# Chunk attention and a bilinear layer on one core: DMA turns ahead of later loads, the sums of weights spread out, the start and block 0's outputs rearranged

## The chip, the cores and the metric

The kernel runs on one core of one Trainium2 chip. The metric is device time in microseconds (us); less is better. A run is one execution of the whole program, and the time given for a kernel is the median of its runs.

The names of the engines in the profile are PE (TensorE, matrix products; PEld are its weight loads), DVE (VectorE), ACT (ScalarE), POOL (GpSimd) and SP (SyncE, whose queue issues every DMA of this kernel).

## The reference

```python
scores = scale * np.matmul(q_c, k_c.transpose(0, 1, 2, 4, 3))   # q, k, v: (8, 8, 576, 64), chunks of 64
attn = np.exp(scores - np.max(scores, axis=-1, keepdims=True))
attn = attn / (np.sum(attn, axis=-1, keepdims=True) + 1e-09)
x = np.matmul(attn, v_c)   # back to (8 batches * 576, 8 heads * 64) = (4608, 512)
a = x @ w_a                # (512, 1536)
b = x @ w_b
out = (a * b) @ w_out      # (4608, 1536) @ (1536, 512), float32
```

Attention is within chunks of 64 positions. Its result, 4608 tokens of 512 values, goes through a layer in which two products are multiplied with each other.

## The kernel before

**Tiles.** The 4608 tokens are 9 blocks of 512 (`NBLK`), a block is two units of 256 tokens (`NU` = 18). Unit u belongs to block u // 2. Units 0 and 1 are done in a way of their own at the start ("half" and "quad" helpers).

**A unit's attention.** `load_natural` brings q, k and v as float32, half a MB each, to `f32[u % 3]`, in two DMAs for a tensor (four for units 8 and 9, whose chunks are of different batches). `cast_qk` and `cast_v` make bfloat16 on GpSimd (`qkb[u % 2]`, `vb[u % 3]`). Then q and k must be turned, so that the head dimension lies on the partitions: for most units by one DMA, `transpose_dma` (line 215), to `qkT[u % 3]`; for units 2 and 3 by TensorE products with the identity (`transpose_pairs`, line 193), with copies out of PSUM by VectorE (q) and ScalarE (k). On TensorE follow `scores` (line 233), `sums` (line 250) and `values` (line 266). ScalarE does the exponential (line 244), the logarithm of the sums (line 276) and the exponential of its negative (line 280); VectorE multiplies the two (`normalise`, line 285) into `xT`, three buffers by block.

**A slot.** `slot(uv, us)` (line 660) puts the sums and values of unit uv and the scores of unit us between the products of a block. What of it runs on ScalarE and VectorE waits in a list `late`, from which `step` takes one entry per step of the block and `drain` all.

**A block's layer.** `ffn(K, ft)` is one step: 4 products with `wb` and 4 with `wa` for one of 12 tiles of 128 columns (line 397), then a copy by ScalarE (line 408) and the product of both by VectorE (line 409). For block 1, steps 0 to 6 are done in halves, first for unit 2, then for unit 3. In blocks 0 and 1 each of four output tiles takes 12 products (line 419), a copy by VectorE (line 429) and a store (line 435). Blocks 2 to 8 use `outs_fast` (line 466) instead, seven products of half width in place of eight for a pair of tiles. It needs sums of the weights, made once on GpSimd by `sum_wo` (lines 453 to 456, six calls), and sums of the products, made by VectorE in each block (`sum_ab`, lines 462 to 464). Both are kept in the buffer `wsta`, through whose ten parts the weights were loaded: the sums of weights in parts 0 to 3, those of products in parts 4 to 7; output weights 0 to 5 lie in parts 4 to 9.

**Order.** The order of every engine's work is the order of the program, written out by hand from line 521 on; nothing reorders it. SP's queue takes loads, turns and stores in program order too; a DMA waits there for its buffer or its data, and all that follows waits with it. Around the change the program has, before: at the end of block 0 cast and turn of unit 4, k and v of unit 5, all of unit 6, cast of unit 5; the turn of unit 5 and the load of unit 7 in the first half steps of block 1; the turn of unit 6 and the load of unit 8 behind step 8, the turn of unit 7 and the load of unit 9 behind output tile 1. The slots are (3, none), (none, 4), (4, 5) behind step 10 of block 1, (5, 6) behind its output tile 1, and from block 2 on one behind step 1 and one behind step 8.

PSUM has four single banks F that `nextF` gives out in a ring, and the pairs PS (scores) and PA (values).

Of the kernel before, what the change touches and what calls it, by code (L numbers as in the profile page):

```python
# [11 lines left out]
def kernel(  # L12
# [10 lines left out]
    nc = tc.nc  # L23
# [11 lines left out]
    DM = H * D  # L35
# [71 lines left out]
    def nextF():  # L107
        return ring("f", F)
# [193 lines left out]
    def quad_cast(m, x, eng):  # L302
        c = (m % 2) * 512
        copy(
            eng,
            qkb[m // 2][:, x, c:c + 512].rearrange("p (r h d) -> p h r d", r=4, h=2),
            f32[m // 2][x][:, c:c + 512].rearrange("p (h r d) -> p h r d", h=2, r=4),
        )

    def quad_turn(m, x, eng):  # L310

        t = nextF().bitcast(BF16)
        c0 = (m % 2) * 512
        for r in range(4):
            c = r * 128
            nc.tensor.transpose(
                t[:, c:c + 128], qkb[m // 2][:, x, c0 + c:c0 + c + 128], identity
            )
        n = 8 * x + 4 * (m % 2)
        dst = qkT[m // 2][:, n:n + 4, :]  # L320
        if x == 0:
            copy(eng, dst, t[:, 0:512].rearrange("p (r t) -> p r t", r=4))
        else:
            copy(
                eng,
                dst.rearrange("p a b -> p (a b)").rearrange("p (t r) -> p t r", r=4),
                t[:, 0:512].rearrange("p (r t) -> p t r", r=4),
            )
# [95 lines left out]
            stop=(ft == NFT - 1),  # L424
        )

    def out_close(K, tg, o):
        t = ring("o", osb)
        nc.vector.tensor_copy(out=t, in_=o)  # L429
        store(K, tg, t)  # L430

    def store(K, tg, t):
        for p, n, b, s0 in runs(2 * K + tg // 2, tg % 2):
            r0 = b * S + s0
            nc.sync.dma_start(out=out[r0:r0 + n, :], in_=t[p:p + n, :])

    def outs(K, tgs):
        o = [nextF() for _ in tgs]
# [27 lines left out]
    def outs_fast(K, t):  # L466
        c = t * 128
        m3, m4, w, y1, y2 = [part[:, t, n, :] for n in range(5)]
        oa, ob = ring("o", osb), ring("o", osb)
        V, A, G = nc.vector, nc.scalar, nc.gpsimd  # L470

        def product(a, b, o=None, pairs=range(NP)):
            o = nextF()[:, 0:HF] if o is None else o
            for i in pairs:
                nc.tensor.matmul(  # L475
                    o, a(i)[:, c:c + 128], b(i), start=(i == 0), stop=(i == NP - 1)
                )
# [35 lines left out]
    def fill(n):  # L513

        for _ in range(n):
            nc.tensor.matmul(PA[:, 0, :], zero[:, 0:128], zero, start=True, stop=True)

    staged = {}

# [1 line left out]
    with tc.manual_schedule():  # L521
# [87 lines left out]
        half_sums(1, 1, PS)  # L609
        half_log(PS)  # L610
        half_inverse(1, 0)
        half_inverse(1, 1)
        cast_v(0, G, 2)
        half_values(0)
        for mm in range(2):
            half_normalise(0, mm)
        land_half("b", 0, 0, G)
# [12 lines left out]
        land_half("a", 0, 1, G)  # L630


        def load_unit(u, xs=(0, 1, 2)):
            if u < NU:
                for x in xs:
                    load_natural(u, x, (q, k, v)[x], nc.sync)

        def cast_unit(u, xs=(0, 1, 2)):
            if u < NU:
                for x in xs:  # L640
                    if x < 2:
                        cast_qk(u, x, G)
                    else:
                        cast_v(u, G)

        def turn_unit(u):
            if u < NU:
                transpose_dma(u, nc.sync)

        def turn_pairs(u, x, engs):  # L650
# [87 lines left out]
        out_close(0, 3, o)  # L738
        slot(None, 3, True)
        drain()  # L740
        cast_unit(4)
        turn_unit(4)
        load_unit(5, (1, 2))
        load_unit(6)
        cast_unit(5)

        for ft in range(7):
            step()
            ffn(1, ft, (0,))
            if ft == 1:  # L750
                slot(3, None, short=True)
            if ft == 3:
                turn_unit(5)
                load_unit(7)
        for ft in range(7):
            step()
            ffn(1, ft, (1,))
            if ft == 3:
                slot(None, 4)
                cast_unit(6)  # L760
        for ft in range(7, NFT):
            step()
            ffn(1, ft)
            if ft == 8:
                turn_unit(6)
                load_unit(8)
                sum_wo(1, G)
            if ft == 10:
                slot(4, 5)
                sum_wo(2, G)  # L770
                cast_unit(7)
        for tg in range(4):
            step()
            outs(1, (tg,))
            if tg == 1:
                slot(5, 6)
                turn_unit(7)
                load_unit(9)
                for i in range(3, NP):
                    sum_wo(i, G)  # L780
        for K in range(2, NBLK):
            for s in range(NFT + 2):
                step()
                if s < NFT:
                    ffn(K, s)
                    if s % 2:
                        sum_ab(s // 2)
                else:
                    outs_fast(K, s - NFT)
                for s0, u in ((1, 2 * K + 3), (8, 2 * K + 4)):  # L790
                    if s == s0 and u - 1 < NU:
                        slot(u - 1, u if u < NU else None)
                    if s == s0 + 1:
                        cast_unit(u + 1)
                    if s == s0 + 3:
                        turn_unit(u + 1)
                        load_unit(u + 3)


# [28 lines left out]
```

## Time and profile before

| | us |
|---|---|
| median of 8 runs | 326.84 |
| lowest, highest | 325.60, 329.06 |
| the profiled execution | 329.06 |
| its span in the trace | 327.3 |
| PE busy in it | 310.3 |
| DVE, ACT, POOL busy in it | 184.5, 132.9, 124.8 |

How to read the profile: a line of a timeline has the start in us, how long the group lasts, the engine, the line of the kernel, the operation, the operands and how many instructions the group has; in brackets stands the idle time of the engine just before, and what ended it. A line of the windows has for each stretch its length, each engine's busy time with the number of its instructions, the granted share of TensorE's clock, the busy share of the DMA engines and their GB/s. A line of a DMA queue (SPq) tells when the queue began with the DMA and how long it was busy issuing it; the data land later. The row of digits of the page has 40 slices of 8.2 us each.

### The profile page before, as it was taken

The numbers are of one execution on the slowest core, as the hardware profiler recorded it, in microseconds if no ns is written. First come the engines' busy times: TensorE is split into PE (matmuls) and PEld (weight loads), VectorE is DVE, ScalarE is ACT, GpSimd is POOL, SyncE is SP. The second block draws the span as 40 slices with busy tenths as digits, with TensorE's granted clock in tenths as the row PEclk, the third lists the DMA queues.
The fourth block names the chain that finished last, engine by engine and source line by source line (L and its number), as shares of the span: only waits on it lengthen the run. The fifth ranks groups of instructions, "written<-read, shape, count | busy, mean of one in ns | idle before, by whom it ended". The sixth has DMA issues, their size and how long they took to land.

```text
span 327.3 us, 7303 instructions
## 1 busy us (share of the span) xinstructions
PE 310.3 (95%) x2910; PEld 178.1 (54%) x2910; DVE 184.5 (56%) x369; ACT 132.9 (41%) x224; POOL 124.8 (38%) x161
## 2 busy tenths in 40 slices
PE   7599999996996999999999999999999999999994
PEld 3334446862442448644854485458545844684474
DVE  3433435532343566596569647875787467646662
ACT  3623216643144353356244614461546163513320
POOL 3657857327993302810281039003900400050022
PEclk9879999997897899999999999999999999999999
DMA  7999999999878999599159917991510110011003
GB/s 233 255 322 386 398 276 255 276 220 247 189 179 201 221 231 231 177 229 239 51 151 237 212 39 133 251 226 65 153 44 0 67 66 0 2 65 66 0 1 128
DMA packets 145698, 55.00 MB, mean 168 GB/s; under 512 B 126208, under 2 KB 139520, under 8 KB 145664
## 3 DMA queue, kind: packets, MB, share of 16 engines
q1 hardware_dynamic: 145664, 54.54, 65.6%
q8 instruction: 22, 0.36, 0.5%
q14 instruction: 12, 0.10, 0.1%
HBM read 37.75 MB, written 9.44 MB: 144 GB/s over the span
## 4 chain that ended last, share of the span: by engine, by line
PE 71%; DMA 13%; SPq 9%; POOL 3%; issue 1%; DVE 1%; POOLq 0%; DVEq 0%
PE F L397 46%; PE F L475 19%; SPq L123 5%; DMA wst<-in_moe_w_a_dram 5%; DMA f<-in_k_dram 3%; DMA f<-in_v_dram 2%; SPq L153 2%; PE F L419 2%; DMA qkT<-qkb 2%; PE PS L233 1%; PE F L250 1%; DMA f<-in_q_dram 1%; SPq L146 1%; PE PA L266 1%; POOL wst L453 1%
## 5 line engine op out<-in xcount | busy, mean ns | idle before, releaser
L397 PE MATMUL F<-xT,wb 128*128 128x512 bf16 (+1 forms) x460 | 116.3, 375 | 0.9 <-DVE xT L383 0.9
L397 PE MATMUL F<-xT,wa 128*128 128x512 bf16 (+1 forms) x460 | 115.3, 373 | 0.2 <-POOL wa L171 0.2
L409 DVE TENSOR_TENSOR ab<-F,bsb 128x512 bf16<-128x512 f32 (+1 forms) x115 | 75.3, 656 | 63.8 <-PE F L397 57.2
L408 ACT CAST bsb<-F 128x512 bf16<-128x512 f32 (+1 forms) x115 | 64.0, 558 | 113.8 <-PE F L397 112.8
L397 PEld LDWEIGHTS <-wa 128*128 128x128 bf16 x460 | 45.4, 99 | 50.8 <-issue 3.6
L397 PEld LDWEIGHTS <-wb 128*128 128x128 bf16 x460 | 44.4, 99 | 47.1 <-issue 4.1
L493 POOL TENSOR_TENSOR part<-part 128x256 f32<-128x256 f32 x14 | 10.1, 724 | 144.6 <-ACT part L501 144.6
L171 POOL CAST qkb<-f 128x1024 bf16<-128x1024 f32 (+1 forms) x37 | 35.5, 975 | 23.3 <-DMA f<-in_q_dram 12.3
L475 PEld LDWEIGHTS <-wst 128*128 128x128 bf16 x420 | 41.1, 98 | 4.8
L475 PE MATMUL F<-wst 128*128 128x256 bf16 x252 | 33.6, 273 | 0.0
L285 DVE TENSOR_TENSOR xT<-PA,inv 128x512 bf16<-128x512 f32 x32 | 21.8, 684 | 15.2 <-ACT inv L280 15.2
L493 DVE TENSOR_TENSOR osb<-F,part 128x256 f32<-128x256 f32 x56 | 22.3, 420 | 10.7 <-POOL part L493 10.4
L171 POOL CAST vb<-f 128x1024 bf16<-128x1024 f32 (+2 forms) x22 | 20.2, 919 | 11.4 <-DMA f<-in_v_dram 8.8
L493 POOL TENSOR_TENSOR part<-part,osb 128x256 f32<-128x256 f32 x28 | 19.7, 725 | 12.2 <-DVE osb L493 12.2
L276 ACT ACTIVATE lns<-F 128x512 f32<-128x512 f32 x32 | 17.4, 595 | 15.8 <-PE F L250 15.8
L419 PE MATMUL F<-wo,ab 128*128 128x512 bf16 x96 | 22.9, 390 | 0.6 <-DVE osb L429 0.6
L475 PE MATMUL F<-wst,ab 128*128 128x256 bf16 x168 | 22.9, 273 | 0.0
L244 ACT ACTIVATE E<-PS 128x1024 bf16<-128x1024 f32 (+1 forms) x20 | 18.8, 941 | 6.6 <-PE PS L339 4.0
L463 DVE TENSOR_TENSOR wst<-ab 128x512 bf16<-128x512 bf16 x42 | 20.9, 498 | 0.0
L464 DVE TENSOR_TENSOR wst<-ab 128x512 bf16<-128x512 bf16 x42 | 20.9, 497 | 0.0
L475 PE MATMUL F<-wo,wst 128*128 128x256 bf16 x168 | 20.6, 273 | 0.0
L493 DVE TENSOR_TENSOR part<-F,part 128x256 f32<-128x256 f32 x14 | 5.9, 425 | 22.7 <-POOL part L493 22.7
(49 smaller groups left out, 194.4 us busy)
## 6 DMA issues: line engine op xcount, KB each, us to landing
out_dram<-osb SPq DMA_DIRECT2D x32, 256.0 KB, 2.2
f<-in_q_dram SPq DMA_DIRECT2D x28, 256.0 KB, 4.1
f<-in_k_dram SPq DMA_DIRECT2D x28, 256.0 KB, 4.1
f<-in_v_dram SPq DMA_DIRECT2D x28, 256.0 KB, 4.7
wst<-in_moe_w_out_dram SPq DMA_DIRECT2D x6, 512.0 KB, 8.8
wst<-in_moe_w_b_dram SPq DMA_DIRECT2D x5, 512.0 KB, 8.4
wst<-in_moe_w_a_dram SPq DMA_DIRECT2D x5, 512.0 KB, 8.4
f<-in_v_dram SPq DMA_DIRECT2D x16, 128.0 KB, 3.3
```

What stands on the lines that cost most here:

```text
L171: eng.tensor_copy(out=out, in_=in_)
L244: nc.scalar.activation(out=e[:, :, s], in_=PS[:, :, s], func=AF.Exp, scale=scale)
L276: nc.scalar.activation(out=lns[:, cl, :], in_=SU[cl], func=AF.Ln)
L285: nc.vector.tensor_tensor(out=x.rearrange("p m (g c t) -> p c g m t", g=2, c=2)[:, cl], in0=PA[:, cl, :].rearrange(shape, g=2, m=4), in1=i ...
L397: nc.tensor.matmul(bank[:, 0:n], w[ft // 2][ft % 2][:, kt, :], x[:, kt, us[0] * 256:us[0] * 256 + n], start=(kt == 0), stop=(kt == NKT - 1),)
L408: nc.scalar.copy(out=bT[:, 0:n], in_=banks[0][:, 0:n])
L409: nc.vector.tensor_tensor(out=ab[ft][:, us[0] * 256:us[0] * 256 + n], in0=banks[1][:, 0:n], in1=bT[:, 0:n], op=MULT)
L419: nc.tensor.matmul(o, ab[ft][:, tg * 128:(tg + 1) * 128], wo[ft // 2][:, ft % 2, :], start=(ft == 0), stop=(ft == NFT - 1),)
L463: nc.vector.tensor_tensor(out=y[:, 0:2], in0=a[:, 0:2], in1=a[:, 2:4], op=ADD)
L464: nc.vector.tensor_tensor(out=y[:, 2:4], in0=a[:, 1:3], in1=a[:, 0:4:3], op=SUB)
L475: nc.tensor.matmul(o, a(i)[:, c:c + 128], b(i), start=(i == 0), stop=(i == NP - 1))
L493: eng.tensor_tensor(out=out, in0=in0, in1=in1, op=op)
```

## The change

- The loads of a unit are split on SP's queue: q of the next unit goes first, then the DMA turn of the unit before it, then k and v. This holds for the turns of units 5 to 8. The four stores of block 0 go behind the turn of unit 4 and k and v of unit 5.
- The slots move: (none, 4) by one half step forward; (5, 6) is split into (5, none) behind output tile 0 of block 1 and (none, 6) behind step 0 of block 2; in block 2, (6, 7) stands behind step 4 and (7, 8) behind step 9.
- The sums of weights: 0 and 1 behind slot (none, 4), ahead of the casts of unit 6; 2 and 3 ahead of the casts of unit 8; 4 and 5 behind cast and turn of unit 8.
- In block 0's outputs the turns of units 2 and 3 by TensorE stand within the products of tiles 2 and 3, and slot (none, 2) behind tile 2.
- At the start, inverse, values and normalising of the first half unit stand ahead of the sums of the second, and four matmuls on zeros (`fill`) to a spare bank are added.
- In the last block the last tile pair's second store is split in two halves of 256 columns; the first half is stored as soon as it is there.

The core of the diff:

```diff
@@ outs_fast
+        halves = K == NBLK - 1 and t == 1
+        if halves:
+            store(K, 2 + t, ob, 0, HF)
...
-        store(K, 2 + t, ob)
+        store(K, 2 + t, ob, HF if halves else 0)
@@ start
         expo(1, 0)
+        half_inverse(0, 0)
+        half_inverse(0, 1)
...
+        cast_v(0, G, 2)
+        land_half("b", 0, 0, G)
         quad_scores(3)
         expo(1, 1)
-        half_inverse(0, 0)
-        half_inverse(0, 1)
+        half_values(0)
+        for mm in range(2):
+            half_normalise(0, mm)
         half_sums(1, 0, PS)
...
+        spare = F[2]
+        fill(1, spare)
         ffn_products(0, 0, (0, 1), (0, 1), B0, "b")
+        fill(2, spare)
         half_values(1)
...
+        fill(1, spare)
         ffn_products(0, 0, (0, 1), (0, 1), B0, "a")
@@ outputs of block 0
-        turn_pairs(2, 0, (V,))
-        out_close(0, 0, o[0])
-        turn_pairs(2, 1, (A,))
-        out_close(0, 1, o[1])
+        stores = [out_close(0, tg, o[tg], False) for tg in range(2)]
         o = nextF()
         for ft in range(NFT):
             out_products(2, ft, o)
             if ft == 5:
-                slot(None, 2, True)
-                drain()
-        slot(2, None)
-        out_close(0, 2, o)
-        sum_wo(0, G)
+                turn_pairs(2, 0, (V,))
+                turn_pairs(2, 1, (A,))
+        slot(None, 2, True)
+        drain()
+        stores.append(out_close(0, 2, o, False))
         o = nextF()
         for ft in range(NFT):
             out_products(3, ft, o)
-            if ft == 3:
+            if ft == 4:
+                slot(2, None)
                 turn_pairs(3, 0, (V,))
                 drain()
-            if ft == 6:
+            if ft == 7:
+                nextF()
                 turn_pairs(3, 1, (A,))
-        out_close(0, 3, o)
+        stores.append(out_close(0, 3, o, False))
         slot(None, 3, True)
         drain()
         cast_unit(4)
         turn_unit(4)
         load_unit(5, (1, 2))
-        load_unit(6)
+        for d in stores:
+            store(*d)
+        load_unit(6, (0,))
         cast_unit(5)
+        turn_unit(5)
+        load_unit(6, (1, 2))
+        load_unit(7, (0,))
@@ block 1, behind the half steps
+        for i in range(2):
+            sum_wo(i, G)
+        cast_unit(6)
+        turn_unit(6)
+        load_unit(7, (1, 2))
+        load_unit(8, (0,))
+        cast_unit(7, (0, 1))
         for ft in range(7, NFT):
             step()
             ffn(1, ft)
...
             if ft == 10:
                 slot(4, 5)
...
+        turn_unit(7)
+        load_unit(8, (1, 2))
+        load_unit(9, (0,))
+        cast_unit(7, (2,))
+        for i in range(2, 4):
+            sum_wo(i, G)
+        cast_unit(8, (0, 1))
         for tg in range(4):
             step()
             outs(1, (tg,))
-            if tg == 1:
-                slot(5, 6)
...
+            if tg == 0:
+                slot(5, None)
+        cast_unit(8)
+        turn_unit(8)
+        load_unit(9)
+        for i in range(4, 6):
+            sum_wo(i, G)
+        for K in range(2, NBLK):
+            for s0, u in zip((4, 9) if K == 2 else (1, 8), (2 * K + 3, 2 * K + 4)):
+                slots[K * (NFT + 2) + s0] = u
```

`load_unit`, `cast_unit` and `turn_unit` get a memory (`once`), so that a tensor named a second time is left out. From block 3 on, the order within a block is as before; casts come one step and the turn and the loads three steps behind a slot, which in block 2 puts the turn of unit 9 behind the first two stores of that block.

More of the change, by code (lines that the diff above doesn't have):

```diff
@@ L425, in out_products, with out_close, store @@
         )
-    def out_close(K, tg, o):
+    def out_close(K, tg, o, now=True):
         t = ring("o", osb)
         nc.vector.tensor_copy(out=t, in_=o)
-        store(K, tg, t)
-    def store(K, tg, t):
+        if now:
+            store(K, tg, t)
+        return K, tg, t
+    def store(K, tg, t, c0=0, c1=DM):
         for p, n, b, s0 in runs(2 * K + tg // 2, tg % 2):
             r0 = b * S + s0
-            nc.sync.dma_start(out=out[r0:r0 + n, :], in_=t[p:p + n, :])
+            nc.sync.dma_start(out=out[r0:r0 + n, c0:c1], in_=t[p:p + n, c0:c1])
     def outs(K, tgs):
@@ L510, in outs_fast, with fill @@
         add(V, ob[:, HF:DM], product(of_asum(2), of_wsum(0)), y2)
-        store(K, 2 + t, ob)
-    def fill(n):
+        store(K, 2 + t, ob, HF if halves else 0)
+    def fill(n, bank=None):
         for _ in range(n):
-            nc.tensor.matmul(PA[:, 0, :], zero[:, 0:128], zero, start=True, stop=True)
+            nc.tensor.matmul(
+                PA[:, 0, :] if bank is None else bank, zero[:, 0:128], zero, start=True, stop=True
+            )
     staged = {}
@@ L630, with once @@
         land_half("a", 0, 1, G)
+        done = set()
+        def once(what, u, xs):
+            xs = [x for x in xs if u < NU and (what, u, x) not in done]
+            done.update((what, u, x) for x in xs)
+            return xs
         def load_unit(u, xs=(0, 1, 2)):
-            if u < NU:
-                for x in xs:
-                    load_natural(u, x, (q, k, v)[x], nc.sync)
+            for x in once("load", u, xs):
+                load_natural(u, x, (q, k, v)[x], nc.sync)
         def cast_unit(u, xs=(0, 1, 2)):
[L639 to L644, printed above, removed]
+            for x in once("cast", u, xs):
+                if x < 2:
+                    cast_qk(u, x, G)
+                else:
+                    cast_v(u, G)
         def turn_unit(u):
-            if u < NU:
+            for _ in once("turn", u, (0,)):
                 transpose_dma(u, nc.sync)
@@ L774 @@
             outs(1, (tg,))
-            if tg == 1:
-                slot(5, 6)
[L777 to L780, printed above, removed]
+            if tg == 0:
[5 more added lines that the diff above has]
+            sum_wo(i, G)
+        slots = {}
+        for K in range(2, NBLK):
+            for s0, u in zip((4, 9) if K == 2 else (1, 8), (2 * K + 3, 2 * K + 4)):
+                slots[K * (NFT + 2) + s0] = u
         for K in range(2, NBLK):
@@ L789 @@
                     outs_fast(K, s - NFT)
[L790 to L797, printed above, removed]
+                if (K, s) == (2, 0):
+                    slot(None, 6)
+                i = K * (NFT + 2) + s
+                if i in slots and slots[i] - 1 < NU:
+                    slot(slots[i] - 1, slots[i] if slots[i] < NU else None)
+                if i - 1 in slots:
+                    cast_unit(slots[i - 1] + 1)
+                if i - 3 in slots:
+                    turn_unit(slots[i - 3] + 1)
+                    load_unit(slots[i - 3] + 3)
 _INS = ['q', 'k', 'v', 'moe_w_a', 'moe_w_b', 'moe_w_out']
```

17 lines of the change are left out of this document (1 added, 16 removed).

## The prediction

> **What bounds the kernel now.** I read the page first, then TensorE's timeline, then the same stretches as windows, then the timelines of the DMA queue, GpSimd and ScalarE.
>
> ```profile
> span 327.3 us, 7303 instructions
> ...
> PEclk9879999997897899999999999999999999999999
> DMA  7999999999878999599159917991510110011003
> ```
>
> A slice is 8.2 us. From slice 14 on TensorE has no dip in its clock, and its DMA engines have room. Up to there the DMA engines are full, and the clock dips near 13, 78 and 103 us. TensorE's timeline shows the last two dips:
>
> ```profile
> 75.42 0.41 PE L250 MATMUL F<-E,ones 64*64 64x512 bf16 x4
> ...
> 79.29 0.64 PE L233 MATMUL PS<-qkT 64*64 64x64 bf16 x32 [3.18 <-DMA qkT<-qkb]
> 79.86 1.89 PE L397 MATMUL F<-xT,wb 128*128 128x512 bf16 x4
> ...
> 90.42 5.35 PE L419 MATMUL F<-wo,ab 128*128 128x512 bf16 x24
> 95.61 1.03 PE L397 MATMUL F<-xT,wb 128*128 128x512 bf16 x4
> ...
> 99.16 0.41 PE L250 MATMUL F<-E,ones 64*64 64x512 bf16 x4
> ...
> 102.97 0.64 PE L233 MATMUL PS<-qkT 64*64 64x64 bf16 x32 [3.12 <-DMA qkT<-qkb]
> ...
> 109.64 1.03 PE L397 MATMUL F<-xT,wb 128*128 128x512 bf16 x4
> ...
> 118.36 0.41 PE L250 MATMUL F<-E,ones 64*64 64x512 bf16 x4
> ...
> 119.28 1.04 PE L397 MATMUL F<-xT,wb 128*128 128x512 bf16 x4
> ```
>
> The scores of units 5 and 7 wait for their DMA turns, 3.18 and 3.12 us, and behind each wait four matmuls take 1.89 us instead of 1.03. The windows show that this is the clock:
>
> ```profile
> 9.91:13.32 3.41, 1.74 (x47) 1.12 (x45) 1.81 (x4) 1.74 (x3) 2.50 (x5) 1.00 1.09 261
> 13.32:16.73 3.41, 2.05 (x42) 1.15 (x41) 1.29 (x2) 3.35 (x6) 1.31 (x4) 0.50 0.84 229
> ...
> 20.15:23.56 3.41, 3.19 (x16) 1.26 (x15) 1.38 (x2) 1.44 (x3) 1.79 (x4) 1.00 1.07 376
> ...
> 74.77:78.18 3.41, 1.34 (x40) 0.59 (x38) 0.79 (x2) 2.62 (x4) 1.71 (x2) 1.00 1.21 252
> 78.18:81.59 3.41, 2.30 (x37) 1.14 (x38) 0.59 (x1) 0.00 (x0) 3.41 (x5) 0.50 1.10 247
> ```
>
> A stretch of 3.41 us in which TensorE worked 1.34 us, and one in which it worked 1.74 us, are each followed by a granted clock of 0.50.
>
> **Both stalls, priced.** From 75.42 to 109.64 us TensorE needs 34.22 us. Its work there is three slots, five steps (step 11 of block 1, steps 0 to 3 of block 2) and four output tiles. A slot undisturbed is 119.28 - 118.36 = 0.92 us, a step (118.36 - 109.64) / 5 = 1.74, two tiles 95.61 - 90.42 = 5.19. That makes 2.8 + 8.7 + 10.4 = 21.9 us, so 12.4 us are lost: 79.86 - 75.42 - 0.92 = 3.5 at the first wait, about the same at the second, and the other 5.4 to the halved clock behind them. If both turns land in time, the change is worth these 12.4 us.
>
> On the clock, the Trainium skill (TensorE: Matmul & The Clock Gate, Part 1) says that the clock falls after at least one idle window of about 3.4 us. By that rule waits of 3.2 us would not cost clock, and removing them would bring 7.0 us only and a time near 321. The trace disagrees: windows with 1.34 and 1.74 us of work were followed by 0.50, so I keep 12.4.
>
> **Does the turn of unit 5 land in time?** The DMA queue before:
>
> ```profile
> 57.42 2.67 SPq L435 DMA_DIRECT2D out_dram<-osb  x4
> 60.22 2.87 SPq L215 DMA_TRANSPOSE qkT<-qkb  x1
> ...
> 70.07 2.19 SPq L123 DMA_DIRECT2D f<-in_k_dram  x2
> ...
> 74.17 3.02 SPq L215 DMA_TRANSPOSE qkT<-qkb  x1
> ...
> 97.44 3.44 SPq L215 DMA_TRANSPOSE qkT<-qkb  x1
> ...
> 110.24 3.34 SPq L215 DMA_TRANSPOSE qkT<-qkb  x1
> ```
>
> Ahead of turn 5 (74.17) stand turn 4, k and v of unit 5 and all of unit 6. The change puts k and v of unit 6 behind it: 74.17 - 70.07 = 4.1 us. The four stores of block 0 go from ahead of turn 4 to ahead of turn 5, which is neutral for turn 5 and brings turn 4 forward by 60.22 - 57.42 = 2.8 us. Who waits for the stores is the first tile of block 1, which reuses their buffers at about 80; issued behind two tensors and a turn, some 7 us later than before, they are out by then. So turn 5 is issued near 70.1 and lands near 79.29 - 4.1 = 75.2. Its own condition, the cast of k of unit 5, is not late:
>
> ```profile
> 67.71 1.04 POOL L171 CAST qkb<-f 128x1024 bf16<-128x1024 f32 x1 [6.03 <-PE F L397]
> ...
> 78.52 1.26 POOL L453 TENSOR_TENSOR wst<-wst 128x512 bf16<-128x512 f32 x1
> ...
> 85.03 2.02 POOL L171 CAST qkb<-f 128x1024 bf16<-128x1024 f32 x2
> ```
>
> It moves 2.8 us forward with its load, to about 65, done at 66. TensorE reached those scores at 79.29 - 3.18 = 76.1 and will be 0.6 us earlier (below): 75.5. That is a margin of 0.3 us only, so turn 5 is the likeliest late one. Turn 4 gains 2.8 us on a need that moves forward by one half step (under 1 us) and those 0.6.
>
> **The later turns.** At the loaded rate a tensor of a unit costs 2.05 us of queue and a turn 3.0 (rows 70.07, 74.17). Turn 6, behind turn 5, k and v of 6 and q of 7, is issued at 70.1 + 3.0 + 4.1 + 2.05 = 79.3 and lands 5.1 us later (74.17 to 79.29), at 84.4; its scores now come after all four tiles and step 0, 75.5 + 0.4 + 1.7 + 10.4 + 0.5 + 1.7 = 90.2. Turn 7 comes 9.15 us behind it, at 88.5, lands at 94.0 (5.5 us, 97.44 to 102.97), and is needed after step 4 at 98. Turn 8 stands behind turn 7, two tensors of unit 8, q of 9 and four stores. Before, turn 7 with a whole load and two stores took 110.24 - 97.44 = 12.8 us; with two stores more (1.3 by the first row) turn 8 is issued at 102.6 and lands at 108, needed after step 9 at 107.7. This reading is slow, as the DMA engines are less full by then; I price it at nothing and keep up to 1 us for the range.
>
> Turn 9 now comes behind the first two stores of block 2, which wait for VectorE, and unit 11's load stands behind it on that queue. Its scores come one fast tile and two steps later:
>
> ```profile
> 124.63 9.17 PE F L475 x84
> ```
>
> Two tiles take 9.17 us, so 4.6 + 3.5 = 8.1 us are left for a turn of 5.1.
>
> On GpSimd two sums of weights take 85.03 - 78.52 = 6.5 us. Sums 0 and 1 now stand ahead of the casts of unit 6: behind the cast of v of unit 5 (two us after its k, near 68) to 75, while k of unit 6 lands near 75.2 + 2.05 = 77, so they hide. Sums 2 and 3 stand ahead of the casts of unit 8, whose k lands after turn 7, near 96; they begin when v of unit 7 has landed, near 84.4 + 4.1 = 88.5, and hide too. Sums 4 and 5 stand behind the casts of unit 8, done near 99 (v lands 4.1 us after turn 7): finished by 106, needed by the first fast tile, two steps and a slot's rest after 107.7, at 112. Cover 6 us.
>
> **Block 0's outputs.**
>
> ```profile
> 45.47 0.62 PE L193 MATMUL F<-identity,qkb 128*128 128x128 bf16 x8 [0.21 <-DVE qkb L171]
> 46.66 1.46 PE L419 MATMUL F<-wo,ab 128*128 128x512 bf16 x6 [0.57 <-DVE osb L429]
> ...
> 54.23 0.64 PE L233 MATMUL PS<-qkT 64*64 64x64 bf16 x32
> ```
>
> ```profile
> 50.47 1.08 ACT L276 ACTIVATE lns<-F 128x512 f32<-128x512 f32 x2 [0.71 <-PE F L250]
> ...
> 53.26 1.07 ACT L169 COPY qkT<-F 128x512 bf16<-128x512 bf16 x2 [0.61 <-PE F L193]
> ```
>
> Six products of tile 2 move ahead of unit 2's turn and cover both waits, 0.78 us together. Then ScalarE becomes the limit: its chain from the logs of unit 2 to its copy for unit 3 ends at 54.33, the scores follow it (54.23), and it had only 0.61 us of idle that an earlier turn on TensorE can remove. I take 0.6 us, between 0 and 0.8.
>
> **The start.** Reordering and four fill matmuls (0.22 us each, 5.19 / 24 by the tiles above) keep TensorE busy. It gains nothing:
>
> ```profile
> 22.38 0.61 POOL L171 CAST wa<-wst 128x512 bf16<-128x512 f32 x1 [0.73 <-DMA wst<-in_moe_w_a_dram]
> ```
>
> ```profile
> 23.05 1.04 PE L397 MATMUL F<-xT,wa 128*128 128x512 bf16 x4 [0.22 <-POOL wa L171]
> ```
>
> At 23.05 TensorE already waits for a weight half cast from a load that nothing in the change moves. Whatever is saved ahead of it becomes idle time there: 0 to 0.2 us, taken as 0.
>
> **The end.** The last store becomes half as large.
>
> ```profile
> out_dram<-osb SPq DMA_DIRECT2D x32, 256.0 KB, 2.2
> ...
> out_dram<-osb SPq DMA_DIRECT2D x8, 128.0 KB, 2.4
> ```
>
> Landing hardly depends on size in these rows; halving could bring 0 to 1.1 us. I take 0.2, near the lower end. [...]
>
> **The sum.** The profiled execution took 329.06 us, 1.76 over its span and 2.2 over the median of 326.84. 329.06 - 12.4 - 0.6 - 0.2 = 315.9 us. Since the executions shown differ by 3.5 us, about one dip of the clock, I read the median as having one dip less in some executions. What is left after the change has neither of the two later dips, so I forecast 315.9 itself and do not subtract the 2.2 again.
>
> **The rivals.**
>
> *A new dip at the start* (0.2). TensorE now idles about 1.5 us more in the stretch that before was 20.15 to 23.56 with 3.19 us of work; 1.7 would be left, like the 1.74 that was followed by a halved clock. 6.8 us at half clock (13.32 to 20.15) cost 3.4 us, less 0.2 that block 0 no longer waits: 319.1. Against it: its matmuls are full-sized, while those of 9.91 to 13.32 were small, and the stretches may fall otherwise.
>
> *A turn is still late* (0.17), unit 5's or unit 8's. The margins are 0.3 and -0.3; 1 to 2 us of wait remain, under the 1.7 us of idle that threw the clock: 317 to 318.
>
> *Unit 7's turn is late as before* (0.05), through GpSimd's casts behind sums, or because the queue's limit is bytes: half of the 12.4 stays, 322.
>
> *The sums behind unit 8's casts hold the block up* (0.04), the slower side. The sums of products that VectorE makes from step 1 of block 2 write the weights' old staging buffer, which sums 4 and 5 read. If the buffer counts as a whole, VectorE waits from 93 until 106 and TensorE, with banks for two more steps, some 9.5 us, plus a dip of 3.4: 315.9 + 12.9 = 328.8. It makes the kernel slower once TensorE's wait exceeds 326.84 - 315.9 - 3.4 = 7.5 us. Against it, casts read parts of that buffer while loads into others are in flight:
>
> ```profile
> 16.64 8.47 DMA wst<-in_moe_w_a_dram
> ```
>
> ```profile
> 21.04 0.61 POOL L171 CAST wb<-wst 128x512 bf16<-128x512 f32 x1 [2.29 <-DMA wst<-in_moe_w_b_dram]
> ```
>
> **How the numbers follow.** The forecast has 0.54. Its own range is 314.6 (0.2 more at the start, 0.2 at block 0 and 0.9 at the end) to 317 (one wait of 1 us). With the dip at the start and a late turn the range reaches 319.6 and leaves out some 0.1. A measurement of this kernel can tell about 0.5% from no change, 1.6 us. All cases but the last are below 325.2: faster 0.95; between, 0.02; slower 0.03.
>
> **What would show it.** Right: TensorE's waits list no turn over 0.5 us, the clock row has no dip after slice 3, unit 5's turn lands near 75, steps 2 and 3 of block 2 take 1.74 us each. Wrong: a granted clock of 0.50 between 23 and 31 us; scores waiting at 75 or 107 us; VectorE waiting for GpSimd's sums near 93; ScalarE holding unit 3's scores past 54.

## The result and the profile after

| | before | after |
|---|---|---|
| median, us | 327.36 (32 runs) | 319.57 (11 runs) |
| lowest to highest | 323.93 to 329.47 | 317.71 to 321.52 |
| profiled execution, its span | 329.06, 327.3 | 319.57, 317.6 |

The ratio after to before is 0.9775, with an interval from 0.9747 to 0.9804: 2.3% faster. The forecast was 315.9 in a range from 314.6 to 319.6. The direction was right. Of the 13.2 us forecast from the profiled execution (329.06 to 315.9), 9.5 came; in medians, 7.8 came where 326.84 to 315.9 would be 10.9. 319.57 stands at the very edge of the range.

The page of the changed kernel, its clock row:

```profile
span 317.6 us, 7309 instructions
...
PEclk9789999999999999999999999999999999999999
```

The dips at 78 and 103 us are gone; the one at the start is still there. TensorE's timeline after:

```profile
22.96 1.04 PE L397 MATMUL F<-xT,wa 128*128 128x512 bf16 x4 [0.29 <-POOL wa L171]
...
53.89 0.60 PE L397 MATMUL F<-xT,wb 128*128 128x256 bf16 x4
...
64.49 0.45 PE L233 MATMUL PS<-qkT 64*64 64x64 bf16 x32 [0.80 <-DMA qkT<-qkb]
...
76.75 0.44 PE L233 MATMUL PS<-qkT 64*64 64x64 bf16 x32 [0.69 <-DMA qkT<-qkb]
...
101.44 1.02 PE L397 MATMUL F<-xT,wa 128*128 128x512 bf16 x4 [0.31 <-DVE ab L409]
...
110.52 0.41 PE L250 MATMUL F<-E,ones 64*64 64x512 bf16 x3 [0.70 <-DVE ab L409]
```

In place of two waits over 3 us stand four under 1 us: the turns of units 4 and 5 are still late, and in block 2 there are two waits that were not there before, for VectorE. The windows give the price by stage. For the kernel before, block 1, block 2 and, as an undisturbed block, block 3:

```profile
54.80:95.61 40.81, 37.63 (x412) 22.63 (x405) 15.20 (x29) 17.90 (x33) 27.73 (x32) 0.92 0.99 225
95.61:133.64 38.03, 34.91 (x318) 19.88 (x317) 20.94 (x43) 14.54 (x24) 11.94 (x15) 0.91 0.94 219
133.64:165.56 31.92, 31.92 (x318) 19.00 (x316) 21.91 (x44) 14.42 (x24) 10.34 (x13) 1.00 0.68 166
```

The same three windows of the changed kernel:

```profile
53.89:89.95 36.06, 34.58 (x379) 21.47 (x373) 15.52 (x29) 16.99 (x32) 18.07 (x20) 1.00 1.08 238
89.95:124.06 34.11, 33.10 (x350) 19.41 (x349) 25.86 (x43) 15.37 (x25) 25.26 (x28) 1.00 0.97 215
124.06:155.98 31.92, 31.92 (x318) 18.99 (x316) 21.59 (x44) 14.43 (x24) 10.43 (x13) 1.00 1.04 228
```

The first number behind the stretch is its length; then come the busy times of TensorE, its weight loads, VectorE, ScalarE and GpSimd with their counts, TensorE's mean clock, the share of the DMA engines and GB/s. Both blocks together fall from 78.84 to 70.17 us, 8.7 us. After the change block 1 would take 34.4 us without waits (the experiments show it) and block 2 31.9 plus the 0.4 for unit 6's scores, which moved into it, so 32.3. That leaves 1.7 us in block 1 and 1.8 in block 2; of the latter 1.0 shows as idle time of TensorE (34.11 less 33.10) and the rest as longer busy time. In block 2 VectorE is busy 25.9 us instead of 20.9, with the same 43 instructions. That is the row to follow.

### The profile page after: what moved, and what is told of

The parts are those of the page before. It is cut to its first block, busy times and chain, and to the rows that moved or that the text cites. A ratio compares the mean times of both kernels' runs of the same rounds, so it can differ in the third digit from the quotient of the medians.

```text
span 317.6 us, 7309 instructions
## 1 busy us (share of the span) xinstructions
PE 306.0 (96%) x2914; PEld 176.7 (56%) x2914; DVE 189.2 (60%) x369; ACT 132.7 (42%) x224; POOL 126.8 (40%) x161
## 4 chain that ended last, share of the span: by engine, by line
PE 64%; DVE 1%; issue 0%; POOL 0%; POOLq 0%; DVEq 0%
PE F L397 41%; PE F L477 20%; PE F L250 1%; PE PA L266 1%; PE PS L233 1%; DVE wst L465 0%; DVE osb L495 0%; POOL part L495 0%; POOLq L856 0%; DVE ab L409 0%; DVE wst L466 0%; DVE wst L464 0%; DVEq L495 0%
## 5 line engine op out<-in xcount | busy, mean ns | idle before, releaser
L397 PE MATMUL F<-xT,wa 128*128 128x512 bf16 (+1 forms) x460 | 112.5, 366 | 0.6 <-DVE ab L409 0.3
L397 PE MATMUL F<-xT,wb 128*128 128x512 bf16 (+1 forms) x460 | 113.1, 368 | 0.0
L397 PEld LDWEIGHTS <-wb 128*128 128x128 bf16 x460 | 43.6, 98 | 44.6 <-POOL wb L171 0.5
L466 DVE TENSOR_TENSOR wst<-ab 128x512 bf16<-128x512 bf16 x42 | 23.3, 554 | 0.0
L276 ACT ACTIVATE lns<-F 128x512 f32<-128x512 f32 x32 | 17.4, 595 | 12.4 <-PE F L250 12.4
L465 DVE TENSOR_TENSOR wst<-ab 128x512 bf16<-128x512 bf16 x42 | 22.5, 535 | 0.0
L419 PE MATMUL F<-wo,ab 128*128 128x512 bf16 x96 | 21.9, 379 | 0.0
```

The lines of the kernel that those rows point to most:

```text
L276: nc.scalar.activation(out=lns[:, cl, :], in_=SU[cl], func=AF.Ln)
L397: nc.tensor.matmul(bank[:, 0:n], w[ft // 2][ft % 2][:, kt, :], x[:, kt, us[0] * 256:us[0] * 256 + n], start=(kt == 0), stop=(kt == NKT - 1),)
L419: nc.tensor.matmul(o, ab[ft][:, tg * 128:(tg + 1) * 128], wo[ft // 2][:, ft % 2, :], start=(ft == 0), stop=(ft == NFT - 1),)
L465: nc.vector.tensor_tensor(out=y[:, 0:2], in0=a[:, 0:2], in1=a[:, 2:4], op=ADD)
L466: nc.vector.tensor_tensor(out=y[:, 2:4], in0=a[:, 1:3], in1=a[:, 0:4:3], op=SUB)
```

## The experiments

Each kernel below is the changed kernel with the edit shown, unless it says otherwise. Ratios are against the kernel before in the same session.

### What the gain is made of

**The queue's order undone**, all else as changed:

```diff
-        load_unit(6, (0,))
+        load_unit(6)
         cast_unit(5)
         turn_unit(5)
-        load_unit(6, (1, 2))
-        load_unit(7, (0,))
+        load_unit(7)
...
```

(the same for the turns of units 6, 7 and 8.)

> The changed kernel with k and v of units 6, 7, 8 and 9 ahead of the turns of units 5, 6, 7 and 8 again; slots and all else as changed. My theory: turns land 4.1 us later. For unit 5 that is a wait of 0.7 + 4.1 = 4.8 us and a dip of the clock of 2.7 us; unit 7's turn then lands near 99.4 and is needed after 105, so no second wait: 6.8 us slower than the change (326, ratio near 0.998). Rival: bytes and not order limit the queue, the turn is as late either way: no slower than the change.

Measured: 325.24 us, ratio 0.9886 (0.9857 to 0.9915). A row of TensorE's timeline in it:

```profile
80.25 0.65 PE L233 MATMUL PS<-qkT 64*64 64x64 bf16 x32 [4.74 <-DMA qkT<-qkb]
```

Its window of block 1:

```profile
53.84:95.61 41.77, 36.73 (x379) 22.14 (x373) 15.52 (x29) 16.99 (x32) 25.95 (x30) 0.92 1.02 230
```

The wait of 4.7 us and one dip (mean clock 0.92 in that stretch) are as expected; block 1 is 5.7 us longer, the time 5.7 us higher than the changed kernel's, 1.1 less than expected. The order of the queue is what took the first wait away. No second long wait appears: block 2 begins at 95.61 as in the kernel before, and turn 7 at 95.99 instead of 97.44, but unit 7's scores now stand behind step 4, come at 105.56 and do not wait.

**The slots undone**: (5, 6) behind tile 1, block 2's behind steps 1 and 8.

```diff
-            if tg == 0:
-                slot(5, None)
+            if tg == 1:
+                slot(5, 6)
...
-            for s0, u in zip((4, 9) if K == 2 else (1, 8), (2 * K + 3, 2 * K + 4)):
+            for s0, u in zip((1, 8), (2 * K + 3, 2 * K + 4)):
...
-                if (K, s) == (2, 0):
-                    slot(None, 6)
```

> The changed kernel with slot (5, 6) behind output tile 1 and the slots of block 2 behind steps 1 and 8 again. My theory: the queue's order is what removes the long waits; the turn of unit 6 lands near 85.5 and would be needed at 84.6, that of unit 7 lands near 95.3 and would be needed near 95: waits of 0.5 to 1.5 us in all, no dip of the clock, 0.5 to 1.5 us slower than the change. Rival: the later slots are what removes the second stall; then a wait of 3 us or more for unit 7's turn comes back with a dip of the clock, 5 to 6 us slower than the change.

Measured: 319.70 us, ratio 0.970 (0.9648 to 0.9753).

```profile
84.42 0.45 PE L233 MATMUL PS<-qkT 64*64 64x64 bf16 x32 [0.26 <-DMA qkT<-qkb]
...
94.16 0.45 PE L233 MATMUL PS<-qkT 64*64 64x64 bf16 x32
...
108.31 0.45 PE L233 MATMUL PS<-qkT 64*64 64x64 bf16 x32 [0.57 <-DMA qkT<-qkb]
```

Units 6 and 8 wait 0.3 and 0.6 us, unit 7 not at all, and the loss of 0.5 to 1.5 us that was expected can't be seen in the time (317.47 to 322.69 in four executions). With the order of the queue changed, the later slots bring nothing that can be seen. So the second long wait does not need both to go: it is gone here with the new order and the old slots, and it was gone in the run before with the old order and the new slots.

**The dips covered, the waits kept**, on the kernel before:

```diff
                 values(uv)
+                if uv in (4, 6):
+                    for _ in range(14):
+                        nc.tensor.matmul(PS[:, 0, :], zero[:, 0:128], zero, start=True, stop=True)
```

> The kernel before with 14 matmuls on zeros, 3.0 us, between the values and the scores in slots (4, 5) and (6, 7), where it waits 3.2 and 3.1 us for the turns. The waits stay, TensorE is busy meanwhile. My theory, by which 5.4 us of the two stalls are the clock: no dip at 78 and 102 us, steps and tiles behind at full speed, up to 5.4 us faster than before where an execution had both dips, 3 to 5 in the median, ratio 0.984 to 0.991. Rival: waits of this length do not cost clock, or the fills only push the scores back: no gain, ratio 0.997 to 1.005.

Measured: 326.25 us, ratio 0.9972 (0.9938 to 1.0006): by time the rival's figure, and 3 to 5 us missed. The timeline shows that the mechanism is there all the same:

```profile
77.53 3.20 PE L670 MATMUL PS<-zero 128*128 128x512 bf16 x14
80.71 0.45 PE L233 MATMUL PS<-qkT 64*64 64x64 bf16 x32
81.09 1.04 PE L397 MATMUL F<-xT,wb 128*128 128x512 bf16 x4
81.96 1.03 PE L397 MATMUL F<-xT,wa 128*128 128x512 bf16 x4
...
90.00 0.45 PE L233 MATMUL PS<-qkT 64*64 64x64 bf16 x32 [1.21 <-DMA qkT<-qkb]
```

Its windows of blocks 1 and 2:

```profile
56.29:95.57 39.28, 38.07 (x427) 23.09 (x420) 15.20 (x29) 17.90 (x33) 23.36 (x27) 1.00 0.96 220
95.57:130.88 35.31, 35.20 (x331) 20.34 (x330) 22.10 (x43) 14.54 (x24) 13.41 (x16) 1.00 1.00 231
```

Behind the filled wait four matmuls take 1.04 us instead of 1.89, and no dip follows either wait. The two blocks take 74.59 us instead of 78.84, 4.25 less; with the 1.2 us that TensorE now waits for unit 6's turn, since it reaches those scores early, that is 5.5, close to the 5.4 that the prediction gave to the clock. Two things keep it out of the time. One is that new wait. The other is that the median execution of the kernel before loses less to the clock than the profiled one: of the 17 executions of it beside this run, 10 have a mean clock of 0.976 or more, while the three dips of the profiled one make 0.969. So 5.4 us was the price of the dips in that execution, not in the median. How many of the change's 7.8 us in the median are clock this run bounds only loosely, since part of what it won was given back.

**The start undone** (old order, no added fills):

```diff
-        half_inverse(0, 0)
-        half_inverse(0, 1)
         quad_cast(3, 0, G)
...
-        spare = F[2]
-        fill(1, spare)
...
```

> The changed kernel with the start in its old order and without the four added fills. My theory: TensorE waits at 23.0 us for a weight half cast from a load that no edit moves, so the start is worth nothing: ratio to the kernel before as the whole change has it, 0.977, and in the profile the matmuls of that weight half start between 22.9 and 23.1 us. Rival: the start brings a dip of the clock less, 3.4 us; then this kernel takes about 323 us (0.988) and the weight half's matmuls start near 26 us.

Measured: 319.41 us, ratio 0.9717 (0.9682 to 0.9753).

```profile
23.75 1.04 PE L397 MATMUL F<-xT,wa 128*128 128x512 bf16 x4 [0.29 <-POOL wa L171]
```

The weight half sets the pace here too; it came 0.8 us later in this execution, and the time is the same. The start is worth nothing that these runs can see.

**Block 0's outputs undone:**

```diff
-        stores = [out_close(0, tg, o[tg], False) for tg in range(2)]
+        turn_pairs(2, 0, (V,))
+        stores.append(out_close(0, 0, o[0], False))
+        turn_pairs(2, 1, (A,))
+        stores.append(out_close(0, 1, o[1], False))
...
```

> The changed kernel with the turns of units 2 and 3 among block 0's output tiles as before (its stores still deferred). In the changed profile block 1 begins 0.9 us earlier than before, but the scores of unit 4 then wait 0.8 us for their DMA turn, and those of unit 5 0.7 us. My theory: the turn of unit 4 sets the time, so undoing this part costs nothing (at most 0.3 us); block 1 begins near 54.8 and the waits for the turns of units 4 and 5 together shrink by about the 0.8 us that block 0 loses. Rival (the forecast's term): 0.6 to 0.9 us slower, waits unchanged.

Measured: 319.96 us, ratio 0.9735 (0.9694 to 0.9775). Block 1 begins at 55.23 us, and its window:

```profile
55.23:89.59 34.36, 34.36 (x380) 21.43 (x373) 15.09 (x29) 16.88 (x32) 18.32 (x20) 1.00 1.11 243
```

TensorE is busy all of these 34.36 us: the waits for both turns are gone, 1.7 us of them, and block 2 begins at 89.59 instead of 89.95. The time shows no loss. Why the waits are gone this execution can't say: block 1 begins 1.3 us later than in the changed kernel's profile, but turns 4 and 5 also begin 2.0 and 2.5 us earlier, at 56.57 and 68.80 instead of 58.53 and 71.34.

### Where the rest went

**Four of six sums of weights left out:**

```diff
-        for i in range(2, 4):
-            sum_wo(i, G)
...
-        for i in range(4, 6):
-            sum_wo(i, G)
...
+        nc.vector.memset(wsum[:, 2:6], 0.0)
         cast_pairs(2, 1, V)
```

> The changed kernel without the sums of weights 2 to 5 on GpSimd; their place is filled with zeros by VectorE at about 43 us, so the outputs of blocks 2 to 8 lack these weights. In the changed profile VectorE's sums of products take 0.9 us instead of 0.4 while GpSimd sums, VectorE falls behind, and TensorE waits for it in block 2 (0.3 and 1.1 us between 100 and 110 us). My theory: GpSimd's sums slow VectorE down; without them VectorE's sums take 0.42 us except beside casts, TensorE's waits for VectorE in block 2 go, 1.3 to 1.8 us faster than the change. Rival: VectorE is late because the slots moved to steps 4 and 9; then the waits stay and nothing is gained.

Its four executions scatter from 316.53 to 358.82 us, so the ratio (0.9804, 0.9733 to 0.9874) decides nothing; the trace does. The last instruction of sum 3 of weights on GpSimd's timeline of the changed kernel, and the first sum of products on VectorE's:

```profile
97.25 0.90 POOL L458 TENSOR_TENSOR wst<-wst 128x256 bf16<-128x256 f32 x1
...
94.94 0.90 DVE L464 TENSOR_TENSOR wst<-ab 128x256 bf16<-128x256 bf16 x1
```

In the kernel before, the last instruction of GpSimd's last sum (sum 5), and VectorE's first sum of products:

```profile
97.41 0.73 POOL L456 TENSOR_TENSOR wst<-wst 128x256 bf16<-128x256 f32 x1
...
100.12 1.11 DVE L462 TENSOR_TENSOR wst<-ab 128x256 bf16<-128x256 bf16 x1
```

Before, the sums were done ahead of VectorE's; after the change sums 3, 4 and 5 run beside them, until 109.6 us. VectorE's groups between 94 and 112 us, in the changed kernel:

```profile
L409 DVE TENSOR_TENSOR ab<-F,bsb 128x512 bf16<-128x512 f32 x9 | 5.9, 679 | 1.6 <-PE F L397 1.5
L465 DVE TENSOR_TENSOR wst<-ab 128x512 bf16<-128x512 bf16 x5 | 4.5, 901 | 0.0
L466 DVE TENSOR_TENSOR wst<-ab 128x512 bf16<-128x512 bf16 x5 | 3.7, 731 | 0.0
```

and between 92 and 110 us in this one:

```profile
L409 DVE TENSOR_TENSOR ab<-F,bsb 128x512 bf16<-128x512 f32 x9 | 6.1, 687 | 3.6 <-PE F L397 3.6
L465 DVE TENSOR_TENSOR wst<-ab 128x512 bf16<-128x512 bf16 x5 | 2.1, 417 | 0.0
L466 DVE TENSOR_TENSOR wst<-ab 128x512 bf16<-128x512 bf16 x5 | 2.1, 416 | 0.0
```

Its window of block 2:

```profile
88.74:121.15 32.41, 32.25 (x347) 19.23 (x349) 21.16 (x43) 15.38 (x25) 10.56 (x12) 1.00 0.90 214
```

The number behind the busy time of a group is its mean duration: 901 ns against 417 in line 465. Block 2 takes 32.41 us instead of 34.11, with the slots where the change put them, so the slots are not why VectorE is late. GpSimd's sums beside VectorE's sums are the 1.7 us. The Trainium skill (SBUF — State Buffer, "SBUF: two separate sides") says that VectorE and GpSimd have one pair of ports in common, which an operation of VectorE with two inputs in SBUF and a reading GpSimd operation hold in turn, each for its whole length. The rows agree: the sums of products have two such inputs and take about twice as long, and GpSimd's half-width sums of weights rise from 0.72 to as much as 0.91 us there, while VectorE's products of line 409 (one input in PSUM) keep their 0.68. The runs show that the sums slow each other; that a port is the reason is the Trainium skill's account.

**Turns earlier:** q of unit 5 behind the turn of unit 4, block 0's stores behind the turn of unit 5.

```diff
-        load_unit(5, (0,))
...
-        load_unit(5, (1, 2))
-        for d in stores:
-            store(*d)
+        load_unit(5)
         load_unit(6, (0,))
         cast_unit(5)
         turn_unit(5)
+        for d in stores:
+            store(*d)
```

> The changed kernel with q of unit 5 behind the turn of unit 4 and the stores of block 0 behind the turn of unit 5. My theory: the queue is limited by bytes ahead; turn 4 lands about 2 us earlier and turn 5 about 2.5 us earlier than in the changed profile (62.4 and 74.2), the scores of units 4 and 5 wait no more; 1.5 us faster than the change if VectorE's waits in block 2 stay as they are. Rival: SP's queue then stands at turn 4 until k of unit 4 is cast and the DMA engines run dry; the turns land as late as now, no gain.

Measured: 320.24 us, ratio 0.9782 (0.9746 to 0.9817): no gain. Blocks 1 and 2:

```profile
55.14:89.49 34.35, 34.09 (x374) 21.38 (x374) 15.42 (x29) 16.89 (x32) 16.93 (x18) 1.00 1.00 233
89.49:124.97 35.48, 33.12 (x346) 19.41 (x348) 25.93 (x43) 15.38 (x25) 24.86 (x28) 1.00 0.97 209
```

Block 1 takes 34.35 instead of 36.06, 1.7 us less; block 2 takes 1.4 us more, with VectorE as busy as in the changed kernel (25.93) and TensorE earlier at the same late sums. That the edit itself takes block 1's waits away this run alone doesn't show: the run with four sums left out has 34.35 there too, without the edit. The pair of runs with the late cast, further down, does.

**Sums in GpSimd's waits**, one by one between the casts of units 5 to 7:

```diff
+        sum_wo(0, G)
+        cast_unit(5, (0,))
+        sum_wo(1, G)
         cast_unit(5)
...
```

> The changed kernel with the six sums of weights on GpSimd set one by one into its waits for loads, the last ahead of the casts of unit 8. My theory: all sums are done by about 95 us, when VectorE's sums of products begin, so those take 0.42 us except beside casts, and TensorE's waits for VectorE in block 2 shrink to under 0.5 us: 1 to 1.5 us faster than the change. Rival: sums ahead of k's casts hold up the turns of units 5 to 7, and what is won in block 2 is lost there.

Measured: 319.59 us, ratio 0.9753 (0.9701 to 0.9805): no gain either. VectorE's waits are gone, but GpSimd's timeline shows the next:

```profile
116.07 1.04 POOL L171 CAST vb<-f 128x1024 bf16<-128x1024 f32 x1 [3.60 <-DMA f<-in_v_dram]
117.08 0.72 POOL L495 TENSOR_TENSOR part<-part 128x256 f32<-128x256 f32 x1
```

and TensorE's:

```profile
118.31 1.33 PE L477 MATMUL F<-wst 128*128 128x256 bf16 x6 [2.07 <-DVE part L495]
119.43 2.55 PE L477 MATMUL F<-wst,ab 128*128 128x256 bf16 x11
```

GpSimd stands 3.6 us at the cast of v of unit 9, the fast tile's sum stands behind that cast, and TensorE waits 2.1 us, with a dip of its clock (eleven matmuls take 2.55 us, 1.36 in the changed kernel). Block 2 takes 36.73 us.

**Both together:**

> Both edits, the earlier turns of units 4 and 5 and the sums in GpSimd's waits. My theory: the two losses are independent, so this is 2.5 to 3.3 us faster than the change, near 316.5 us, which is the forecast's 315.9 but for the smaller waits. Rival: one loss hides the other, 1.5 us at most.

Measured: 321.77 us, ratio 0.9829 (0.9779 to 0.9878), the same wait at 119.04, 2.7 us long. The edits' gains do not add; neither the theory nor the rival had this third wait in its numbers.

**The cast of unit 9 behind the first fast tile**, with both repairs, and with the sums alone:

```diff
-                if i - 1 in slots:
-                    cast_unit(slots[i - 1] + 1)
+                if i - (3 if (K, s) == (2, 12) else 1) in slots and (K, s) != (2, 10):
+                    cast_unit(slots[i - (3 if K == 2 and s == 12 else 1)] + 1)
```

> The kernel with earlier turns and sums in GpSimd's waits, and the cast of unit 9 moved behind the first fast tile of block 2 (its turn behind it). In the run without that move, block 2's fast tiles took 13.4 us instead of 9.2: GpSimd stood at the casts of unit 9, whose k and v land near 111 and 116, and the fast tile's sums stood behind them, with a dip of the clock. My theory: that is where the two earlier repairs went; with the cast out of the way the fast tiles take 9.2 us and the kernel is 3 to 4 us faster than the change, 316 us, the forecast's time. Rival: the byte-limited queue only moves the wait on, now to the turn of unit 9 or block 3's scores (a wait of 2 us or more near 125 us), 319 to 320.

> Sums in GpSimd's waits and the late cast of unit 9, without the earlier turns of units 4 and 5. My theory: as the run with all three but for the waits of units 4 and 5, which differ from execution to execution between 0 and 1.7 us: 316 to 318. Rival as for the run with all three.

Measured: 319.75 us, ratio 0.9761 (0.9715 to 0.9806), and 318.96, 0.9739 (0.9696 to 0.9782). By time the rivals have it. The two runs differ only in the earlier turns of units 4 and 5, and both executions have no clock dip at the start: block 1 takes 34.34 us with the earlier turns and 36.16 without, where the waits of 0.8 us for turns 4 and 5 stand as in the changed kernel. So the earlier turns are worth 1.8 us in block 1. In the first run block 2 takes 34.45 us, and these two waits hold it:

```profile
108.37 0.45 PE L233 MATMUL PS<-qkT 64*64 64x64 bf16 x32 [0.76 <-DMA qkT<-qkb]
...
121.86 0.81 PE L477 MATMUL F<-wst 128*128 128x256 bf16 x6 [0.97 <-DVE part L495]
```

Unit 8's turn landed at 108.3 to 108.5 us in this run and in the two before it, though block 2 began up to 1.9 us earlier than in the changed kernel; in the second run, where turn 4 had begun as late as 58.32, it landed at 110.2. It is not a fixed time: with four sums left out unit 8's scores began at 108.11 without a wait. The moved casts now stand between the two fast tiles. The queue bears on the first: the changed kernel's SP timeline from turn 7 to turn 8.

```profile
90.03 3.21 SPq L215 DMA_TRANSPOSE qkT<-qkb  x1
93.29 2.64 SPq L123 DMA_DIRECT2D f<-in_k_dram  x4
95.97 2.67 SPq L123 DMA_DIRECT2D f<-in_v_dram  x4
98.68 2.68 SPq L123 DMA_DIRECT2D f<-in_q_dram  x4
101.47 3.40 SPq L437 DMA_DIRECT2D out_dram<-osb  x4
104.97 2.75 SPq L215 DMA_TRANSPOSE qkT<-qkb  x1
```

Units 8 and 9 are loaded in quarters of 128 KB, each 0.67 us of the queue's time; q of unit 9 and four stores, 6.3 us together, stand ahead of turn 8.

**Turn 8 ahead of them**, with the earlier turns and the sums in GpSimd's waits, and of unit 9 only v cast behind the fast tiles (the edit beyond those two repairs):

```diff
         load_unit(8, (1, 2))
-        load_unit(9, (0,))
...
         cast_unit(8, (0, 1))
+        turn_unit(8)
...
-        cast_unit(8)
-        turn_unit(8)
         load_unit(9)
+        cast_unit(8)
```

> Earlier turns of units 4 and 5 and sums in GpSimd's waits, and now the turn of unit 8 ahead of block 1's stores and of q of unit 9, and the cast of v of unit 9 behind block 2's fast tiles. In all runs so far the turn of unit 8 landed at 108.3 us or later, whatever was gained ahead of it. My theory: the queue's stretch with units 8 and 9, 24 loads of 128 KB at 0.68 us of issue each, is what the gains run into; now the turn lands near 104, the scores of unit 8 do not wait, the fast tiles take 9.2 us, block 3 begins near 120.6 as forecast, 316 us. Rival: GpSimd's casts or VectorE hold block 2 up in any case; block 3 begins at 122 or later, 318 to 320.

Measured: 317.27 us (316.52 to 318.06), ratio 0.9684 (0.9642 to 0.9726). Its interval lies below the changed kernel's. Blocks 1 and 2:

```profile
54.59:88.94 34.35, 34.35 (x378) 21.39 (x373) 15.44 (x29) 16.89 (x32) 26.84 (x31) 1.00 1.01 237
88.94:121.46 32.52, 32.52 (x350) 19.26 (x349) 21.39 (x43) 15.38 (x25) 12.82 (x15) 1.00 0.98 210
```

TensorE has no wait in either. Turn 8 begins at 100.09 and lands at 104.6. From 78.84 us before both blocks are at 66.87: 12.0 us, the 12.4 of the forecast but for 0.4. Block 3 begins 0.9 us later than expected, and the time is 1.3 us above the 316 expected. This version beats both kernels. Turn 8 ahead was run only together with the other repairs; what it is worth alone is not shown.

## Why the prediction was right and wrong

**Right: the mechanism and its bulk.** The waits of units 5 and 7 and the dips behind them were the loss. k and v of unit 6 ahead of turn 5 made the first (the run with the order undone brings back 4.7 us of wait and one dip); filling the waits in the kernel before gave 5.5 us of clock in the two blocks; and the whole is 12 us large (the last run). The start is worth nothing that its run can show, and the end 0.2 us in the two profiles: from VectorE's last sum to the end of the span 2.99 us before, 2.78 after.

**The step that failed: "if both turns land in time, the change is worth these 12.4 us", taken whole.** Blocks 1 and 2 gave 8.7. Two terms priced at nothing cost 1.7 us each, and a third gain was lost again. Turns 4 and 5 in the changed kernel's queue:

```profile
58.53 3.89 SPq L215 DMA_TRANSPOSE qkT<-qkb  x1
...
71.34 3.26 SPq L215 DMA_TRANSPOSE qkT<-qkb  x1
```

- *The turn of unit 5*, margin 0.3 us, was late. It began at 71.34 instead of 70.1, behind a turn 4 that began at 58.53, 1.1 us later than assumed. Turn 4 itself, for which no landing was worked out at all, landed near 64.4 where the same reckoning would give 62.4. Together 1.7 us in the profiled execution. It varies: of the eight profiles with this order of the queue up to turn 4, three began that turn between 56.2 and 56.6 us and waited for neither turn 4 nor turn 5. The other five began it between 58.0 and 59.0; in four of them the scores of unit 4 waited 0.3 to 0.8 us, and in the fifth, with the start undone, block 1 itself began 0.8 us later. The rival "a turn is still late" happened, for units 4 and 5. Turn 8 was late too, begun at 104.97 instead of 102.6, but in the changed kernel VectorE's lateness hides it: in the second run with the late cast, where it began at 105.18 and VectorE was in time, its scores waited 0.9 us.
- *The sums of weights*, "hide too" and "cover 6 us". The cover was reckoned against the product that needs the sums and not against the engine that works beside them. Sums 3 to 5 now run while VectorE makes its first sums of products, slow these from 417 to 901 ns (line 465), and cost 1.7 us. No rival named this. The rival of one undivided buffer did not happen: VectorE's first sums ran from 94.94 us, before sums 4 and 5.
- *The 0.6 us of block 0*: 0.8 came there, but in the profiled execution they only brought TensorE earlier to turns 4 and 5, where it waited.

With 0.2 us more outside the span, these make about the 3.7 us between 315.9 and 319.57. That the time still lies within the range is luck: the range reaches that far for a new dip at the start together with a late turn, and the new dip, the likeliest rival, is in none of the profiles. None has a halved clock between 23 us and block 1. In the changed kernel's profile the idle time that the rival counts on was not there either: from 21.82 to 25.20 us TensorE was busy 3.09 of 3.38 us.

**Also off:** that the price of the dips holds for the median. 5.4 us are those of one execution with both dips.

**Still open:** how the 7.8 us in the median divide into waits and clock, and why turn 4 begins about two us later in some executions. The three profiles with the early turn 4 are those of the eight with a clock dip of 10.24 us at the start; what links the two was not tried.

## What to carry to other kernels

Where a queue is full and several engines run close behind it, price a repair by the margin of everything that comes next, not by the wait alone: here the earlier turns won 1.7 us in block 1 and lost 1.4 in block 2, the sums in GpSimd's waits freed VectorE and met a cast that held TensorE 2.1 us, and only with turn 8 moved as well, at the place where they ran into the queue, did the gains come home. Work moved to an idle engine is free only if it doesn't slow the engine beside it; look for an instruction whose mean duration grows while its shape stays. And take the price of a clock dip from the spread of executions, not from the one that was profiled.

## What the runs showed of the hardware

The length of the clock's dips comes in multiples: 3.41, 6.83, 10.24 and 13.65 us in these profiles. How busy TensorE was in the 3.41 us ahead does not alone decide on a dip: 2.15 us of work from 8.17 to 11.58 were followed by a granted clock of 0.50 in the changed kernel, and 2.15 us from 7.42 to 10.83 by a full clock in the run with the start undone. So the prediction's "1.7 us of idle that threw the clock" is no lower bound: here it was 1.26.

At the start, among profiles of the changed kernel's kind, dips of 10.24 us went with block 0's outputs beginning between 39.6 and 40.6 us, none with 39.0 to 39.7: less than 1 us on average for a dip of that length. The weights' loads set the pace there: in the three profiles without a dip at the start TensorE waits 1.6 to 2.2 us for the weights' casts, in the six with the dip of 10.24 us nowhere over 0.2 us, so the dip mostly takes time that would be waited.

A load of 128 KB in 256-byte rows costs the queue 0.67 us of issue. One of 256 KB costs 0.60 at the least (1.20 for two), and up to 1.5 in the changed kernel between 60 and 90 us. At the least, then, the piece and not the byte costs: a tensor in quarters takes 2.7 us of the queue, one in halves as little as 1.2.
